# Windowed attention and a gated feed-forward on one core: the gate taken as a hyperbolic tangent from the exponential's table

## The chip, the cores and the metric

The kernel runs on one core of a Trainium2 chip. The metric is the device time of one execution in microseconds (us); the number given for a kernel is the median of several runs. A core has five engines that work side by side and wait for each other through semaphores: TensorE (PE, matrix products), VectorE (DVE), ScalarE (ACT, functions from a table, copies), GpSimd (POOL) and SyncE (SP, which here issues the transfers). In the profile, PEld is PE's loading of weights, which overlaps its products.

## The reference

Causal attention in a window of 64 positions (8 batches, 8 heads, 576 positions, 64 wide), then a gated feed-forward on 4608 tokens of width 512 with 1536 hidden elements.

```python
scores = np.where(mask, scores, -1000000000.0)
scores = scores - np.max(scores, axis=-1, keepdims=True)
attn = np.exp(scores)
attn = attn / (np.sum(attn, axis=-1, keepdims=True) + 1e-09)
...
gate = 1.0 / (1.0 + np.exp(-(x @ w_gate)))
val = x @ w_val
return (gate * val @ w_out).astype(np.float32)
```

x is the attention's output. The kernel needs two functions from ScalarE's table: the exponential in the softmax and the sigmoid in the gate.

## The kernel before

**Tiling.** The 4608 tokens are 12 token tiles `t` of 384. The attention of a tile is done in four units `(t, p)`, one for each pair of heads `p`. A unit has these steps: loads of q, k (L180, L181) and v (L191); `scores` (L210, PE); `exponentials` (L230), in which for each of two halves and three blocks DVE finds a minimum (L244) and ACT takes an exponential (L252); `normalize` (L262), where DVE takes the reciprocal of the row sums (`invert`, L259 and L260) and POOL or DVE multiplies by it (L269); `stage_b` (L296), in which PE transposes (L301) and ACT copies (L306, tile `pT`); and `outputs` (L325), the product with v (L331).

**Products in two ways.** Tiles 0 and 1 go through `up_gate`, `up_val` and `down`: for each of 12 hidden tiles `j`, PE computes a bank `ph` (L362) for the gate and one for the value, ACT makes the gate `g` from the first (`gate_table`, L371), DVE multiplies the second with it (L395) and splits the result into a high and a low part (L387, L389), and PE adds `down` (L409). There are three banks `ph`, taken in turn: a new bank's product waits until what read the bank three before is done. The other ten tiles go in pairs, in five stages `s`. A stage has six steps `k` of seven products (`product`, L613, matmuls at L586, tile `pr`), whose sums DVE combines (L596, L625); from them again a gate on ACT (L371) and a product on DVE (L629), four of each per step. Then follow the down products `y` (L586 too, from `last_product`), with `h_split` (L668 on ACT, L669 on DVE) ahead of them.

**Weights.** The weights come as 64-bit numbers and are converted in the kernel during the first 180 us: loads L105, on ACT L117, L118 and L158, on DVE L126 to L130 and L159, and stores to DRAM (L154, L448, L457). Sums of weights for the later stages are made on POOL (L508 to L528) from transfers back (L498).

**What sets the order.** The steps are put into a list of planned times, sorted and written out in that order (`put`, `attend`, L705 to L922). The tile framework then schedules each engine's instructions by a simulated timeline. PE's products keep the order of the program (`pe`, L85). ACT's exponentials and gates are held to one common order by `chain` and `table_order` (L88): each is issued after the one before, whichever of the two functions it is. Some steps are held behind a mark by hand (`marks`): exponentials of the first units behind an earlier `pT`; conversions of hidden tile `j` behind `marks[j]`, the last gate or exponential and the last split of an earlier tile; and the rounding of x (L576) behind the last gate.

**Table loads.** ScalarE has one table active at a time. Ahead of an instruction whose function isn't in the active table, the compiler puts a table load, which the profile shows under the line of that instruction: L252 for an exponential, L371 for a gate, L77 for the warm-up at the start.

Of the kernel before, what the change touches and what calls it, by code (L numbers as in the profile page):

```python
# [14 lines left out]
AF = mybir.ActivationFunctionType  # L15
ALU = mybir.AluOpType
# [10 lines left out]
def attn_ffn(ctx: ExitStack, tc: tile.TileContext, qT, kT, vN, w_gate, w_val, w_out, out, outT):  # L27
# [3 lines left out]
    nc = tc.nc  # L31
# [47 lines left out]
    def psum(s, i, nm):  # L79
        return ps_b.tile([P, DM], F32, name=nm, tag=f"b{s % 2}{i}")  # L80

    marks = {"pT": {}}
    chain = []
# [4 lines left out]
    def table_order():  # L88
        return tc.issue_after(chain[-1]) if chain else nullcontext()
# [166 lines left out]

    def invert(rs):

        nc.vector.scalar_tensor_tensor(out=rs, in0=rs, scalar=1e-9, in1=rs, op0=ALU.add, op1=ALU.max)  # L259
        nc.vector.reciprocal(out=rs, in_=rs)  # L260

    def normalize(t, p, h):  # L262
        pt, rs = st[(t, p, h)], sums_of[(t, p)][:, h, :]
        if t < 2 and h:
            nc.vector.reduce_sum(out=rs, in_=pt, axis=mybir.AxisListType.X)
        if t < 4:
            invert(rs)
        eng = nc.vector if t == 3 and p % 2 or t // 2 == 2 else nc.gpsimd
        eng.tensor_mul(out=pt, in0=pt, in1=rs.unsqueeze(2).broadcast_to([P, UP, P]))  # L269
# [21 lines left out]
    def stage_n(t, p):  # L291
        invert(sums_of[(t, p)])
        for h in range(2):
            normalize(t, p, h)
# [58 lines left out]
    def up(t, j, m):  # L353
        ph = h_bank(f"ph{m}_{t}_{j}")
        w2 = wgv[m][j]
        prs = []
        for p in range(NP):
            whi, wlo = (w2[:, p // 2, e, p % 2 * P:(p % 2 + 1) * P] for e in range(2))
            xh, xl = xs[(t, p)][:, 0, :], xs[(t, p)][:, 1, :]
            prs += [(whi, xh), (whi, xl), (wlo, xh)]  # L360
        for i, (l, r) in enumerate(prs):
            pe(nc.tensor.matmul(ph, l, r, start=i == 0, stop=i == len(prs) - 1))  # L362
        return ph
# [3 lines left out]

    def gate_table(t, j, c):
        g = mp.tile([P, TT], F32, name=f"g_{t}_{j}", tag="g", bufs=4)
        with table_order():  # L370
            act = nc.scalar.activation(g, c, AF.Sigmoid)  # L371
        chain.append(act.ins)
        marks["gate"] = act.ins
        gates[(t, j)] = g

    def up_gate(t, j):
        gate_table(t, j, up(t, j, 0))

    def hidden_split(t, j, h32, eng):
        if t == 1 and j < NF - KEEP:  # L380
            pool, tag, bufs = (xp, f"x{10 + j}", 1) if j < 4 else (xp, f"e{j - 4}", 1) if j < 9 else (mp, "raw", RAW)
            h2 = pool.tile([P, 2, TT], F32R, name=f"h2_{t}_{j}", tag=tag, bufs=bufs)
            h_hi, h_lo = h2[:, 0, :], h2[:, 1, :]
        else:
            h_hi = mp.tile([P, TT], F32R, name=f"hh_{t}_{j}", tag="hh", bufs=3)
            h_lo = mp.tile([P, TT], F32R, name=f"hl_{t}_{j}", tag="hl", bufs=3)
        nc.vector.tensor_copy(out=h_hi, in_=h32)  # L387
        hh[(t, j)] = (h_hi, h_lo)
        return eng.tensor_sub(out=h_lo, in0=h32, in1=h_hi.bitcast(F32))  # L389

    def up_val(t, j):
        ph = up(t, j, 1)
        g = gates.pop((t, j))
        h32 = mp.tile([P, TT], F32, name=f"h32_{t}_{j}", tag="c", bufs=CB)
        nc.vector.tensor_mul(out=h32, in0=ph, in1=g)  # L395
        last = hidden_split(t, j, h32, nc.vector)
        if t == 0:
            marks[j] = (chain[-1], last.ins)

    def down(t, j, i, first, last):  # L400
        h_hi, h_lo = hh[(t, j)]
# [28 lines left out]
    gates = {}  # L430
# [152 lines left out]
    def three(ps, w2, q, x2, first, last, check=True):  # L583
        whi, wlo = (w2[:, e, q * P:(q + 1) * P] for e in range(2))
        for i, (l, r) in enumerate(((whi, x2[:, 0, :]), (whi, x2[:, 1, :]), (wlo, x2[:, 0, :]))):
            pe(nc.tensor.matmul(ps, l, r, start=first and i == 0, stop=last and i == 2,  # L586
                                skip_group_check=not check))

    def combine(st, n, nm, emit):


        ps = st[PRODUCTS[n][2]][:, :TT]

        def plus(a, tag, bufs):
            o = mp.tile([P, TT], F32, name=f"{tag}{n}_{nm}", tag=tag, bufs=bufs)
            marks["plus"] = nc.vector.tensor_add(out=o, in0=ps, in1=a).ins  # L596
            return o

        if n == 0:
            st["p1"] = mp.tile([P, TT], F32, name=f"p1_{nm}", tag="p1", bufs=2)  # L600
            nc.scalar.copy(st["p1"], ps)
        elif n == 1:
            st["u2"] = plus(st["p1"], "u", 2)
        elif n == 3:
            emit(1, 1, st[2][:, :TT], plus(st["p1"], "c", CB))
        elif n == 4:
            emit(0, 0, ps, None)
        elif n == 5:
            emit(1, 0, ps, st["p1"])
        elif n == 6:  # L610
            emit(0, 1, ps, st["u2"])

    def product(s, k, n, m):  # L613
        st, b = acc[m], PRODUCTS[n][2]
        if n < 3:
            st[b] = psum(1 + m, b, f"pr{b}_{m}_{s}_{k}")
        for c in range(2):
            three(st[b][:, :TT], wt[(s, k, m, n)], c, xs[(s, n, c)][0], n < 3 and c == 0, c == 1, n < 3)

        def emit(r, b, in0, in1):  # L620
            t, j = 2 * s + b, k + r * NK
            c = in0
            if in1 is not None:
                c = mp.tile([P, TT], F32, name=f"c{n}_{m}_{s}_{k}", tag="c", bufs=CB)
                nc.vector.tensor_add(out=c, in0=in0, in1=in1)  # L625
            if m == 0:
                gate_table(t, j, c)
            else:
                nc.vector.tensor_mul(out=hidden(s, k)[2 * r + b], in0=c, in1=gates.pop((t, j)))  # L629

        combine(st, n, f"{m}_{s}_{k}", emit)

    def hidden(s, k):

        if (s, k) not in ht:
            nm = f"{s}_{k}"

            def one(tag, bufs, i):
                return mp.tile([P, TT], F32, name=f"h{i}_{nm}", tag=tag, bufs=bufs)

            def two(pool, tag, bufs, i):
                h2 = pool.tile([P, 2, TT], F32, name=f"h{i}_{nm}", tag=tag, bufs=bufs)
                return [h2[:, 0, :], h2[:, 1, :]]

            if k < 2:
                h5 = wts.tile([P, 5, TT], F32, name=f"h_{nm}", tag=f"wp_{k}")
                t = [h5[:, i, :] for i in range(5)]
            elif k == 2:
                t = [one("hh", 3, i) for i in range(3)] + [one("hl", 3, i) for i in range(3, 5)]
            else:  # L650
                t = two(mp, "raw", RAW, 0) + two(mp, "raw", RAW, 1)
                if k == 3:
                    t.append(one("hl", 3, 2))
                else:
                    if k == 4:
                        ht[(s, "last")] = two(wts, f"wo_{WOB}", 1, 2)
                    t.append(ht[(s, "last")][k - 4])
            ht[(s, k)] = t
        return ht[(s, k)]
# [66 lines left out]
    for n in range(2 * NP):  # L726
        t, p = divmod(n, NP)
# [32 lines left out]
    for i, (kind, t, j) in enumerate(plan):  # L760
        attend(i)
        at[(kind, t, j)] = now
        if (kind, t, j) == ("up", 0, 0):
            now = -9.9
        if kind == "up":
            put(now, 9, up_gate, t, j)
            now += UPT / 2
            attend(i + 0.5)
            put(now, 9, up_val, t, j)
            now += UPT / 2  # L770
        else:
            for x in range(TB):
                put(now + x * DPT, 9, down, t, j, x, j == 0, j == NF - 1)
            now += DNT
        if (kind, t, j) == ("up", 0, 0):
            now = 0.0
    for i in range(KINDS * NF):
        j, m = divmod(i, KINDS)
# [125 lines left out]
    for tm, _, f, a in events:  # L904
        if f in (conv_a, conv_b, conv_c):
            with ExitStack() as behind:
# [4 lines left out]
                j, m = divmod(a[0], KINDS)  # L911
# [56 lines left out]
```

## Time and profile before

| what | value |
|---|---|
| median of three runs | 962.8 us (959.86 to 964.3) |
| the profiled execution, and its span | 961.67 us, 959.9 us |
| busy in the span: PE, PEld | 941.3, 898.0 us |
| busy in the span: DVE, ACT, POOL | 714.3, 602.7, 147.5 us |
| mean granted TensorE clock | 0.998 |
| ACT table loads at L371, at L252, at L77 | 40, 39, 1 |
| DMA | 273.45 MB, mean 285 GB/s |

The span runs from the first to the last instruction. A row of the profile's groups reads: line, engine, operation, what is written and read, shapes, count | busy us, mean ns of one | idle time of the engine just before, and what ended it. In a timeline, a row starts with its start and its duration in us, and square brackets hold the idle time of the engine ahead of it. In a list of waits stand the total, the number and the longest.

### The profile page before, as it was taken

Reading aid. Unit: us, or ns where it says so; the run is one execution under the profiler, and the core shown is the slowest. Engines: PE = TensorE matmul, PEld = TensorE weight load, DVE = VectorE, ACT = ScalarE, POOL = GpSimd, SP = SyncE. Lnnn points to the kernel's source line nnn. Section 1 sums busy time; section 2 is a strip of 40 time slices with the busy share of each in tenths; the row PEclk is TensorE's granted clock in tenths of the full one; section 3 lists DMA queues with packets and bytes.
Section 4 is the critical chain, followed back from the end, with each engine's and each line's share of the span. In section 5 each row is a group of like instructions: output and inputs, shape, how many; then the busy total and the mean of one; then the engine's idle time right before and its main releaser. Section 6 shows DMA issues by size and latency. Waiting matters only on the chain.

```text
span 959.9 us, 20420 instructions
## 1 busy us (share of the span) xinstructions
PE 941.3 (98%) x7164; PEld 898.0 (94%) x7164; DVE 714.3 (74%) x1919; ACT 602.7 (63%) x1487; POOL 147.5 (15%) x232
## 2 busy tenths in 40 slices
PE   6899999999999999999999999999999999999998
PEld 5799998879998999999999999999999999999998
DVE  7898989788778985666976576796566697567782
ACT  7878878667677754766755666764666675222350
POOL 4210103703765000110100111100110100000000
PEclk9999999999999999999999999999999999999999
DMA  9899988979988999888889888879988868988464
GB/s 339 304 357 370 347 303 271 347 275 358 369 301 271 402 325 309 277 265 269 251 260 316 267 273 261 270 256 284 302 273 249 268 220 257 314 249 251 143 217 157
DMA packets 105510, 273.45 MB, mean 285 GB/s; under 512 B 11456, under 2 KB 33600, under 8 KB 105408
## 3 DMA queue, kind: packets, MB, share of 16 engines
q1 hardware_dynamic: 105408, 272.15, 84.7%
q8 instruction: 57, 0.93, 0.4%
q14 instruction: 45, 0.37, 0.1%
HBM read 220.20 MB, written 51.90 MB: 283 GB/s over the span
## 4 chain that ended last, share of the span: by engine, by line
PE 77%; ACT 6%; DVE 5%; DMA 5%; issue 3%; POOL 2%; SPq 0%; DVEq 0%; ACTq 0%; POOLq 0%
PE pr L586 42%; PE y L586 23%; PE s L220 3%; PE pp L301 2%; PE ph L362 2%; PE y L409 2%; DMA w32d<-w 2%; PE s L331 2%; ACT p L252 2%; DMA a<-w32d 1%; PE oo L331 1%; DVE w L130 1%; POOL ws L528 1%; ACT L252 1%; ACT raw L118 1%
## 5 line engine op out<-in xcount | busy, mean ns | idle before, releaser
L586 PE MATMUL pr<-x_T,wt 128*128 128x384 f32 x1224 | 227.5, 338 | 0.0
L586 PE MATMUL y<-h,wot 128*128 128x384 f32 x1260 | 219.9, 334 | 0.0
L586 PEld LDWEIGHTS y<-h,wot 128*128 128x128 f32 x1260 | 218.2, 188 | 0.6 <-DVE h L629 0.3
L586 PEld LDWEIGHTS pr<-x_T,wt 128*128 128x128 f32 x1224 | 211.6, 188 | 4.5 <-issue 3.6
L586 PE MATMUL pr<-x_B,wt 128*128 128x384 f32 x1008 | 189.4, 336 | 0.0
L586 PEld LDWEIGHTS pr<-x_B,wt 128*128 128x128 f32 x1008 | 174.7, 188 | 0.8 <-issue 0.5
L668 ACT CAST h<-h 128x384 fp32r<-128x384 f32 x210 | 102.7, 515 | 80.6 <-PE y L586 43.3
L269 POOL TENSOR_TENSOR p<-p,rs 128x384 f32<-128x384 f32 x76 | 66.4, 890 | 551.8 <-DVE rs L260 496.7
L669 DVE TENSOR_TENSOR h<-h,h 128x384 fp32r<-128x384 f32 x210 | 110.7, 554 | 26.8 <-ACT h L668 26.1
L252 ACT ACTIVATE p<-p,mn 128x128 f32<-128x128 f32 x288 | 110.9, 393 | 10.2 <-DVE mn L244 9.7
L362 PE MATMUL ph<-x,w 128*128 128x384 f32 x576 | 107.0, 339 | 1.3 <-ACT g L371 0.8
L362 PEld LDWEIGHTS ph<-x,w 128*128 128x128 f32 x576 | 99.5, 188 | 4.3 <-ACT g L371 1.4
L371 ACT ACTIVATE g<-c 128x384 f32<-128x384 f32 x90 | 46.6, 524 | 66.3 <-DVE c L625 65.9
L244 DVE CUSTOM_DVE_ANT_0 p<-s,m 128x128 f32<-128x128 f32 x288 | 65.3, 284 | 27.6 <-PE s L220 27.5
L629 DVE TENSOR_TENSOR h<-c,g 128x384 f32<-128x384 f32 x90 | 55.5, 616 | 30.2 <-ACT g L371 24.7
L371 ACT ACT_TABLE_LOAD x40 | 51.3, 1283 | 12.7 <-DVE c L625 11.4
L220 PE MATMUL s<-k,q 64*64 64x128 f32 x1152 | 46.5, 293 | 7.2 <-DMA k<-in_kT_dram 5.8
L596 DVE TENSOR_TENSOR c<-pr,p 128x384 f32<-128x384 f32 x60 | 33.0, 550 | 23.7 <-PE pr L586 23.7
L252 ACT ACT_TABLE_LOAD x39 | 50.0, 1283 | 0.7
L252 ACT ACTIVATION_READ_ACCUMULATOR p<-p,mn 128x1 f32 x264 | 49.8, 188 | 0.0
L220 PEld LDWEIGHTS s<-k,q 64*64 64x64 f32 x1152 | 34.2, 141 | 13.9 <-DMA q<-in_qT_dram 5.2
L301 PE MATMUL pp<-ident,p 128*128 128x128 f32 x288 | 42.6, 281 | 4.6 <-POOL p L269 2.6
(106 smaller groups left out, 1215.9 us busy)
## 6 DMA issues: line engine op xcount, KB each, us to landing
wt<-wd SPq DMA_DIRECT2D x186, 512.0 KB, 4.5
wot<-wod SPq DMA_DIRECT2D x105, 512.0 KB, 4.7
v<-in_vN_dram SPq DMA_DIRECT2D x48, 384.0 KB, 5.4
wd<-ws SPq DMA_DIRECT2D x48, 256.0 KB, 4.4
k<-in_kT_dram SPq DMA_DIRECT2D x48, 224.0 KB, 5.2
q<-in_qT_dram SPq DMA_DIRECT2D x48, 192.0 KB, 5.1
w32d<-w SPq DMA_DIRECT2D x36, 256.0 KB, 4.6
wd<-w SPq DMA_DIRECT2D x36, 256.0 KB, 5.8
```

The source lines that it names most:

```text
L220: pe(nc.tensor.matmul(sc[h][half * BLK:(half + 1) * BLK, u, :], qt[h * BLK:(h + 1) * BLK, U * BLK:(U + 1) * BLK], kt[h * BLK:(h + 1) * BLK ...
L244: nc.vector.tensor_tensor_reduce(out=pt[:, u, :], in0=sc[:, u, :], in1=masks[key], op0=ALU.add, op1=ALU.min, scale=-SCALE, scalar=3.0e38, ...
L252: exp = nc.scalar.activation(pt[:, u, :], pt[:, u, :], AF.Exp, bias=mn[:, u:u + 1], scale=-1.0, **sums)
L269: eng.tensor_mul(out=pt, in0=pt, in1=rs.unsqueeze(2).broadcast_to([P, UP, P]))
L301: pe(nc.tensor.transpose(pp[:, u, :], pt[:, u, :], ident))
L362: pe(nc.tensor.matmul(ph, l, r, start=i == 0, stop=i == len(prs) - 1))
L371: act = nc.scalar.activation(g, c, AF.Sigmoid)
L586: pe(nc.tensor.matmul(ps, l, r, start=first and i == 0, stop=last and i == 2, skip_group_check=not check))
L596: marks["plus"] = nc.vector.tensor_add(out=o, in0=ps, in1=a).ins
L629: nc.vector.tensor_mul(out=hidden(s, k)[2 * r + b], in0=c, in1=gates.pop((t, j)))
L668: nc.scalar.copy(h2[:, 0, :], src)
L669: nc.vector.tensor_sub(out=h2[:, 1, :], in0=src, in1=h2[:, 0, :].bitcast(F32))
```

## The change

The gate becomes `AF.Tanh` in place of `AF.Sigmoid`, and one plus the tangent is multiplied with the value in one instruction of DVE (`gated`, a scalar-tensor-tensor: add 1, then multiply) in place of the plain product. For this to be the same number, x must come in half: sigmoid(z) = (1 + tanh(z/2))/2, and gate and value are both linear in x. The half is taken in the softmax: `invert` now takes the reciprocal of twice the sum plus 2e-9. The exponentials stay in `chain`; the gates are taken out of it, so that ACT's order of gates against exponentials is left to the scheduler.

```diff
     def invert(rs):
-        nc.vector.scalar_tensor_tensor(out=rs, in0=rs, scalar=1e-9, in1=rs, op0=ALU.add, op1=ALU.max)
+        nc.vector.scalar_tensor_tensor(out=rs, in0=rs, scalar=2e-9, in1=rs, op0=ALU.add, op1=ALU.add)
         nc.vector.reciprocal(out=rs, in_=rs)
...
     def gate_table(t, j, c):
         g = mp.tile([P, TT], F32, name=f"g_{t}_{j}", tag="g", bufs=4)
-        with table_order():
-            act = nc.scalar.activation(g, c, AF.Sigmoid)
-        chain.append(act.ins)
+        act = nc.scalar.activation(g, c, AF.Tanh)
         marks["gate"] = act.ins
         gates[(t, j)] = g
+
+    def gated(out, val, g):
+        nc.vector.scalar_tensor_tensor(out=out, in0=g, scalar=1.0, in1=val, op0=ALU.add, op1=ALU.mult)
...
-        nc.vector.tensor_mul(out=h32, in0=ph, in1=g)
+        gated(h32, ph, g)
         last = hidden_split(t, j, h32, nc.vector)
         if t == 0:
-            marks[j] = (chain[-1], last.ins)
+            marks[j] = (marks["gate"], last.ins)
...
-                nc.vector.tensor_mul(out=hidden(s, k)[2 * r + b], in0=c, in1=gates.pop((t, j)))
+                gated(hidden(s, k)[2 * r + b], c, gates.pop((t, j)))
```

In the changed kernel the gate stands at L370, the product at L375, and what follows is one line lower or higher than before. ACT keeps the one table load of the warm-up. PE and POOL keep their order; on SP one pair of transfers trades places (a store of weight parts, L448, and a load for the sums, L498).

On ACT around the exponentials of attention unit (4, 2), in the first of the five stages, stood before (`xf` is a tile of x, `p` the scores that become weights, `mn` and `rs` minima and sums, `g` a gate, `c` a combined product):

```order
L285 COPY xf_0_3282<-s_4_2_3269 128x128
L252 ACT_TABLE_LOAD
L252 ACTIVATE p_4_2_3297,rs_2_3299<-p_4_2_3297,mn_4_2_3298 128x128 x3
L288 COPY xf_0_3282<-s_4_2_3268 128x128
L252 ACTIVATE p_4_2_3307,rs_2_3299<-p_4_2_3307,mn_4_2_3308 128x128 x3
L371 ACT_TABLE_LOAD
L371 ACTIVATE g_6_3333<-c_0_1_0_3331 128x384
```

and stand now:

```order
L285 COPY xf_0_3282<-s_4_2_3269 128x128
L252 ACTIVATE p_4_2_3297,rs_2_3299<-p_4_2_3297,mn_4_2_3298 128x128 x3
L288 COPY xf_0_3282<-s_4_2_3268 128x128
L252 ACTIVATE p_4_2_3307,rs_2_3299<-p_4_2_3307,mn_4_2_3308 128x128 x3
L370 ACTIVATE g_6_3333<-c_0_1_0_3331 128x384
```

The two table loads are gone and nothing else moved; this is how it looks in nearly all units. On ACT around the exponentials of unit (2, 3), while the last weights are converted, stood before (`raw` is a loaded weight, `w` a converted one):

```order
L371 ACTIVATE g_9_2273<-ph_0_9_2260 128x384
L158 CAST w_10_2279<-w_1_10_2247 128x2x256
L252 ACT_TABLE_LOAD
L252 ACTIVATE p_2_3_2302,rs_3_2304<-p_2_3_2302,mn_2_3_2303 128x128 x3
L252 ACTIVATE p_2_3_2314,rs_3_2304<-p_2_3_2314,mn_2_3_2315 128x128 x3
L117 ACTIVATE w_0_11_2401<-raw_11_2348 128x512
L118 ACTIVATE raw_11_2348<-raw_11_2348 128x512
L118 ACTIVATE raw_11_2361<-raw_11_2361 128x512
L118 ACTIVATE raw_10_2381<-raw_10_2381 128x512
```

and stand now:

```order
L370 ACTIVATE g_9_2273<-ph_0_9_2260 128x384
L118 ACTIVATE raw_11_2348<-raw_11_2348 128x512
L118 ACTIVATE raw_11_2361<-raw_11_2361 128x512
L118 ACTIVATE raw_10_2381<-raw_10_2381 128x512
L158 CAST w_10_2279<-w_1_10_2247 128x2x256
L117 ACTIVATE w_0_11_2401<-raw_11_2348 128x512
L252 ACTIVATE p_2_3_2302,rs_3_2304<-p_2_3_2302,mn_2_3_2303 128x128 x3
L252 ACTIVATE p_2_3_2314,rs_3_2304<-p_2_3_2314,mn_2_3_2315 128x128 x3
```

Four instructions of the conversion now stand ahead of the exponentials. On DVE at the same unit stood before (`rs` are the sums whose reciprocal is taken, `h` the product with the gate, `hh` and `hl` its parts, `zz` a step of the conversion):

```order
L259 SCALAR_TENSOR_TENSOR rs_3_2304<-rs_3_2304 128x3
L395 TENSOR_TENSOR h_0_9_2338<-ph_0_9_2325,g_9_2273 128x384
L130 ISA w_2_9_2285<-raw_9_2209,w_2_9_2285 128x1024
L260 RECIPROCAL rs_3_2304<-rs_3_2304 128x3
L259 SCALAR_TENSOR_TENSOR rs_3_2304<-rs_3_2304 128x3
L387 CAST hh_9_2340<-h_0_9_2338 128x384
L260 RECIPROCAL rs_3_2304<-rs_3_2304 128x3
L389 TENSOR_TENSOR hl_9_2341<-h_0_9_2338,hh_9_2340 128x384
L126 TENSOR_SCALAR zz_11_2422<-w_0_11_2401 128x512
L128 SCALAR_TENSOR_TENSOR w_0_11_2401<-w_0_11_2401,zz_11_2422 128x512
```

and stand now:

```order
L375 SCALAR_TENSOR_TENSOR h_0_9_2338<-g_9_2273,ph_0_9_2325 128x384
L130 ISA w_2_9_2285<-raw_9_2209,w_2_9_2285 128x1024
L388 CAST hh_9_2340<-h_0_9_2338 128x384
L259 SCALAR_TENSOR_TENSOR rs_3_2304<-rs_3_2304 128x3
L390 TENSOR_TENSOR hl_9_2341<-h_0_9_2338,hh_9_2340 128x384
L126 TENSOR_SCALAR zz_11_2422<-w_0_11_2401 128x512
L260 RECIPROCAL rs_3_2304<-rs_3_2304 128x3
L259 SCALAR_TENSOR_TENSOR rs_3_2304<-rs_3_2304 128x3
L128 SCALAR_TENSOR_TENSOR w_0_11_2401<-w_0_11_2401,zz_11_2422 128x512
L260 RECIPROCAL rs_3_2304<-rs_3_2304 128x3
```

The product with the gate and the conversion come first now, the two reciprocals after them, the second one last. Unit (3, 2) is changed in the same way, with two conversions among the exponentials.

## The prediction

> **What bounds the kernel now.** I read the page first, its busy times.
>
> ```profile
> PE 941.3 (98%) x7164; PEld 898.0 (94%) x7164; DVE 714.3 (74%) x1919; ACT 602.7 (63%) x1487; POOL 147.5 (15%) x232
> ```
>
> TensorE (PE) is busy 98% of the span of 959.9 us, while ScalarE (ACT), the engine that the change relieves, is busy 63%. A share is an average, so I cut the span into stretches: one with the first attention units, one with tiles 0 and 1 and the first stage of products, one with the later product stages, and the end.
>
> ```profile
> 0.00:40.00 40.00, 30.23 (x416) 24.55 (x418) 29.36 (x157) 32.35 (x105) 16.40 (x28) 0.96 0.89 327
> 40.00:320.00 280.00, 274.86 (x2133) 251.93 (x2130) 237.46 (x637) 212.12 (x506) 90.56 (x156) 1.00 0.93 326
> 320.00:920.00 600.00, 600.00 (x4417) 585.59 (x4416) 430.79 (x1094) 347.78 (x856) 40.51 (x48) 1.00 0.83 269
> 920.00:960.00 40.00, 36.22 (x209) 35.90 (x208) 16.74 (x34) 10.49 (x22) 0.00 (x0) 1.00 0.59 197
> ```
>
> After the stretch and its length come the busy times of PE, of PE's weight loads (PEld), VectorE (DVE), ACT and GpSimd (POOL), then PE's clock, the DMA share and GB/s. From 320 to 920 us PE is busy for all of the 600 us. The first 40 us lack 9.8 us, the last 40 us 3.8 us, and the 280 us between them 5.14 us; the clock is full from 40 us on. Matmul ends are modelled, so "all busy" needs a second look. The chain of waits gives it: in that stretch it runs through PE, piece after piece.
>
> ```profile
> 477.50 43.88 PE y L586 x252
> 629.27 43.88 PE y L586 x252
> ```
>
> That is 174 ns a matmul (43.88/252), the same in both, and a stage of 151.8 us from one piece to the next (629.27 - 477.50). So the later stages are bound by TensorE's own work, and the time to be had lies in PE's waits. Last view: PE's waits from 35 us (just ahead of the first gate) to 320 us; none is listed after that.
>
> ```profile
> PE pp L301 <- DVE p L269: 1.9, 3, 1.3
> PE ph L362 <- ACT g L371: 0.8, 2, 0.4
> PE ph L362 <- DVE h L395: 0.6, 1, 0.6
> PE oo L331 <- ACT pT L306: 0.5, 1, 0.5
> PE s L220 <- DMA k<-in_kT_dram: 0.5, 1, 0.5
> PE pp L301 <- POOL p L269: 0.4, 1, 0.4
> PE s L220 <- ACT xf L319: 0.2, 1, 0.2
> ```
>
> Together 4.9 us in ten waits (total, times, longest).
>
> **The change part by part.** First, what leaves and what takes its place:
>
> ```profile
> L371 ACT ACT_TABLE_LOAD x40 | 51.3, 1283 | 12.7 <-DVE c L625 11.4
> L252 ACT ACT_TABLE_LOAD x39 | 50.0, 1283 | 0.7
> L252 ACT ACTIVATE p<-p,mn 128x128 f32<-128x128 f32 x288 | 110.9, 393 | 10.2 <-DVE mn L244 9.7
> L371 ACT ACTIVATE g<-c 128x384 f32<-128x384 f32 x90 | 46.6, 524 | 66.3 <-DVE c L625 65.9
> L629 DVE TENSOR_TENSOR h<-c,g 128x384 f32<-128x384 f32 x90 | 55.5, 616 | 30.2 <-ACT g L371 24.7
> L395 DVE TENSOR_TENSOR h<-ph,g 128x384 f32<-128x384 f32 x24 | 13.2, 550 | 0.1
> L128 DVE SCALAR_TENSOR_TENSOR w<-w,zz 128x512 int32<-128x512 int32 x36 | 25.1, 697 | 0.4
> L159 DVE TENSOR_TENSOR w<-w,w 128x512 fp32r<-128x512 f32 x36 | 25.9, 723 | 2.9 <-ACT w L158 2.9
> ```
>
> 1. *Table loads.* The new order has one, the warm-up's; 40 + 39 = 79 go, 79 x 1.283 = 101 us of ACT. In the 600 us in which PE never waits this buys nothing by itself: it turns into idle time of ACT. It counts where a table load stands ahead of something that PE waits for. I went through the ten waits.
>
> The longest is the 1.3 us one, of attention unit (4, 2) (token tile, head pair):
>
> ```profile
> 285.77 1.28 ACT L252 ACT_TABLE_LOAD   x1
> 289.67 1.28 ACT L371 ACT_TABLE_LOAD   x1
> 286.28 0.08 DVE L244 DVE_READ_ACCUMULATOR2_ANT mn<- 128x1 f32 x1
> 289.69 0.17 DVE L259 SCALAR_TENSOR_TENSOR rs<-rs 128x6 f32<-128x6 f32 x1 [1.33 <-ACT p L252]
> 290.43 0.65 DVE L269 TENSOR_TENSOR p<-p,rs 128x384 f32<-128x384 f32 x1
> 291.52 0.70 DVE L629 TENSOR_TENSOR h<-c,g 128x384 f32<-128x384 f32 x1 [0.45 <-ACT g L371]
> 292.15 0.81 DVE L269 TENSOR_TENSOR p<-p,rs 128x384 f32<-128x384 f32 x1
> 293.10 0.52 PE L301 MATMUL pp<-ident,p 128*128 128x128 f32 x3 [1.28 <-DVE p L269]
> ```
>
> PE's second three transposes wait for the second normalization L269, which stands on DVE behind the gate's product L629, which waits for the gate, which stands behind the second table load; the reciprocal (L259) waits for exponentials that stand behind the first. Without the first, the exponentials can start when the first minimum is there (286.28 + 0.08 = 286.36, against 285.77 + 1.28 = 287.05 for the end of the load), some 0.7 us earlier; without the second the gate follows by another 1.28 us, and DVE would end the second L269 about 1.3 us earlier. PE's own time to reach these transposes is 293.10 - 1.28 = 291.8, so all 1.28 us go, with little to spare.
>
> The wait for L395, at unit (3, 1), goes only in part:
>
> ```profile
> 174.75 0.94 DVE L159 TENSOR_TENSOR w<-w,w 128x512 fp32r<-128x512 f32 x1
> 175.96 0.16 DVE L259 SCALAR_TENSOR_TENSOR rs<-rs 128x3 f32<-128x3 f32 x1 [0.27 <-ACT p L252]
> 176.04 0.55 DVE L395 TENSOR_TENSOR h<-ph,g 128x384 f32<-128x384 f32 x1
> 176.64 2.36 PE L362 MATMUL ph<-x,w 128*128 128x384 f32 x12 [0.55 <-DVE h L395]
> ```
>
> DVE stood for 0.27 us ahead of L259; the rest of the 0.55 us is DVE's own weight conversion. I take 0.27.
>
> The other waits that a table load precedes I cost at their full length: the two gates (0.8), the rest of the L269 row on DVE (1.9 - 1.28 = 0.6), POOL's L269 (0.4) and pT (0.5, its copy is queued behind the first gate). The k load (0.5) and xf (0.2) have none ahead of them and stay. Sum: 1.28 + 0.27 + 0.8 + 0.6 + 0.4 + 0.5 = 3.85 us.
>
> 2. *Order.* On PE and POOL nothing moves. The freed order moves several instructions at two places, units (3, 2) and (2, 3): ACT takes weight conversions ahead of exponentials, DVE takes the reciprocals later. What is queued behind them is POOL's normalization, then PE's transposes; first (3, 2), then (2, 3):
>
> ```profile
> 115.99 1.94 POOL L269 TENSOR_TENSOR p<-p,rs 128x384 f32<-128x384 f32 x2 [14.04 <-DVE rs L259]
> 121.17 0.82 PE L301 MATMUL pp<-ident,p 128*128 128x128 f32 x6
> 153.66 1.94 POOL L269 TENSOR_TENSOR p<-p,rs 128x384 f32<-128x384 f32 x2 [14.90 <-DVE rs L259]
> 160.68 0.82 PE L301 MATMUL pp<-ident,p 128*128 128x128 f32 x6
> ```
>
> They have 121.2 - 117.9 = 3.2 us and 160.7 - 155.6 = 5.1 us to spare. At (2, 3) the second reciprocal is now behind a subtraction (hl), a zz and an L128 more, each at most about 0.7 us by these rows, so some 2 us; at (3, 2) behind the first two of them. On ACT the conversions ahead take the place of the table load that went. I cost the move at nothing; if that cover were gone, every further microsecond would be PE's. The swapped pair on the SP queue (a store of parts and a load for the sums) is costed at nothing for the same reason.
>
> 3. *Gate and product.* No row shows a hyperbolic tangent. The nearest rows are the sigmoid at 524 ns and, at a third of the elements, the exponential, 393 ns with a bias operand: a tangent at either's speed changes nothing, and one twice as slow would cost 144 x 0.52 = 75 us of ACT (144 gates, 12 token tiles by 12 hidden tiles), less than the 101 us set free. The product as a scalar-tensor-tensor: by L128 and L159, 697 against 723 ns at 512 elements, it costs what the plain one did, 550 to 616 ns at 384; I take no difference, with 10% either way, 144 x 0.06 = 9 us of DVE, which has 42 us idle between 40 and 320 us and 169 us after that. The reciprocal keeps its number of instructions.
>
> 4. *What is late next.* PE arrives up to 3.9 us earlier at everything, but weights, sums and k come by DMA, whose share is 0.93 between 40 and 320 us. Some of the time will be waited for there instead. No row gives the amount; it lies between 0 and 3.85 us. As conversions on ACT come earlier as well, I take little, 0.35 us.
>
> **Sum:** 3.85 - 0.35 = 3.5 us. The profiled execution took 961.67 us, its span plus 1.8 us around it: 961.67 - 3.5 = **958.2 us**. That execution lies 1.1 us below the median of the runs shown, 962.8, and inside their spread (959.86 to 964.3); from the median the same sum gives 959.3. A measurement of this kernel tells about 0.5%, 4.8 us, from no change, so the forecast is a gain that lies below that bound.
>
> **The rivals.** *More is hidden than the waits show.* If PE idle on the list is only the visible part, all 5.14 us between 40 and 320 us go. Beyond them there are weight loads that stand idle where PE does not, after 320 us:
>
> ```profile
> PEld s L331 <- issue: 3.7, 15, 0.3
> PEld s L331 <- ACT g L371: 1.5, 6, 0.3
> ```
>
> With the 1.5 us that these owe to the gate, 5.1 + 1.5 = 6.6 us, 955.0 us. For it: each wait also drains PE's pipeline. Against it: the same weight load idles by as much at "issue", with no gate behind it (3.7/15 = 0.25 us, as 1.5/6). [...] I hold the rival at 29%.
>
> *The gain is eaten by DMA.* PE waits for k, weights or sums by what it gained: 961.7 us. For it: the DMA share and the k load on the list. Against it: none of PE's waits after 35 us but 0.5 us is for a transfer. 13%.
>
> *The product is slow.* The one way I see to the other side: DVE takes a scalar-tensor-tensor of floats much slower than the plain product. 24 + 24 products (tiles 0 and 1, and the first product stage) fall between 40 and 320 us, where DVE idles 280 - 237.5 = 42.5 us: 0.89 us each. From there on the excess is PE's, since its banks ph and pr are freed by these products. At three times the plain price, 1.1 us extra, 48 x 0.21 = 10 us less the 3.5: 968.3 us. The pair 697 and 723 ns speaks against it. 6%.
>
> *It doesn't do what it says*, and loads remain in other places: the order of the changed kernel on ACT has a single one, so I leave this out.
>
> **How the numbers follow.** Forecast, 958.2 us: 52%. Hidden gain, 955.0: 29%. Eaten, 961.7: 13%. Slow product, 968.3: 6%. Faster by over 0.5% is the second case, 0.29; within 0.5% the first and the third, 0.65; slower the last, 0.06. The range leaves out the last case and goes from 955.0 to 961.7 us plus what the median lies above the profiled execution, to 963.0.
>
> **What would show it.** ACT: one table load, ACT about 100 us less busy, gates near 520 ns. DVE: products near 550 to 616 ns. PE: of the ten waits only the k load, xf and a part of L395 stand; PE still busy for all of the later stages. The forecast is wrong if the 4.9 us of waits return under other names, above all DMA, or if the stages of 151.8 us become shorter, which would say that a "busy" PE had been held by ACT.

## The result, and the profile after

| | before | after |
|---|---|---|
| median (lowest to highest), us | 962.8 (959.86 to 964.3), five runs | 954.68 (953.44 to 956.07), five runs |
| profiled execution, and its span, us | 961.67, 959.9 | 955.21, 953.4 |
| ratio of the times, 95% interval | 1 | 0.9924 (0.9908 to 0.994) |

The changed kernel is 0.76% faster, 7.3 us by the ratio (0.0076 x 962.8), and the two medians are 8.1 us apart; the interval, 0.6 to 0.92%, lies wholly above the 0.5% bound. The span of the profiled execution is 6.5 us shorter. The forecast was 3.5 us and "within 0.5%". The median lies 0.3 us below the lower end of the range, at the number given for the rival "more is hidden than the waits show". That end was counted from the profiled execution of before, and the profiled execution after, 955.21 us, lies 0.2 us above it.

First the page's busy times after, and its two rows for the gate and the gated product:

```profile
PE 938.2 (98%) x7164; PEld 898.0 (94%) x7164; DVE 721.7 (76%) x1919; ACT 507.0 (53%) x1408; POOL 155.3 (16%) x232
...
L370 ACT ACTIVATE g<-c 128x384 f32<-128x384 f32 x90 | 47.0, 522 | 85.4 <-DVE c L626 79.5
...
L375 DVE SCALAR_TENSOR_TENSOR h<-g,c 128x384 f32<-128x384 f32 x90 | 53.6, 595 | 6.3 <-ACT g L370 0.9
```

ACT has 79 instructions fewer (1487 to 1408) and is 95.7 us less busy. A gate takes 522 ns where the sigmoid took 524, a product 595 ns where the plain one took 616. None of the three explains 6.5 us: ACT was not the bound, and the other two hardly moved.

Next the same cuts of the span as before; columns are the busy times of PE, PEld, DVE, ACT and POOL, then the clock, the DMA share and GB/s.

```profile
0.00:40.00 40.00, 30.23 (x418) 24.63 (x420) 29.81 (x158) 31.79 (x105) 16.41 (x28) 0.96 0.88 327
40.00:320.00 280.00, 278.23 (x2184) 257.57 (x2179) 247.70 (x652) 180.79 (x486) 93.25 (x156) 1.00 0.95 338
320.00:920.00 600.00, 600.00 (x4401) 586.42 (x4401) 433.88 (x1091) 288.18 (x806) 45.65 (x48) 1.00 0.83 266
```

Between 40 and 320 us PE fitted 2184 matmuls in place of 2133, so the gain is made there. Equal stretches of time hold different work, though. A better cut holds the same work: from the product `ph` (L362) that follows PE's wait at 41 us to the start of the first down products `y`, 2139 matmuls in both; first before, then after:

```profile
42.16:325.71 283.55, 278.94 (x2139) 255.90 (x2137) 241.26 (x645) 215.75 (x512) 90.56 (x156) 1.00 0.93 329
```

```profile
41.81:319.62 277.81, 276.29 (x2139) 255.84 (x2137) 245.54 (x647) 179.55 (x483) 93.25 (x156) 1.00 0.95 338
```

This stretch is 5.74 us shorter, and two columns give two accounts of it. By PE its idle time fell from 4.61 to 1.52 us, 3.09 us. By PEld the busy time stayed the same (255.90 and 255.84), and the idle time fell from 27.65 to 21.97 us, 5.68 us: the whole gain.

PE's waits from 35 to 320 us after the change, against the ten (4.9 us) of before:

```profile
PE s L220 <- DMA k<-in_kT_dram: 0.8, 1, 0.8
PE pp L301 <- DVE p L269: 0.5, 1, 0.5
PE oo L331 <- ACT pT L306: 0.3, 1, 0.3
PE s L220 <- ACT xf L319: 0.2, 1, 0.2
```

Every wait for a gate, for the product of a gate and for POOL is gone, and so is the 1.28 us one. The later stages, in the chain of waits after:

```profile
319.62 43.88 PE y L587 x252
471.26 43.88 PE y L587 x252
...
905.78 43.98 PE y L587 x252
```

A stage is now 151.64 us from one piece to the next, against 151.77 before: 0.13 us each, in stages in which PE is "all busy" in both. In all, 6.1 us had been gained when the first `y` begins (325.71 to 319.62), and 0.4 us in what follows: 0.13 us in each of three stages, and nothing in the last one, which takes 131.24 us from `y` to `y` in both.

### The profile page after: what moved, and what is told of

Read it like the earlier page. It is cut to its first block, busy times and chain, and to the rows that moved or that the text cites. A ratio compares the mean times of both kernels' runs of the same rounds, so it can differ in the third digit from the quotient of the medians.

```text
span 953.4 us, 20341 instructions
## 1 busy us (share of the span) xinstructions
PE 938.2 (98%) x7164; PEld 898.0 (94%) x7164; DVE 721.7 (76%) x1919; ACT 507.0 (53%) x1408; POOL 155.3 (16%) x232
## 4 chain that ended last, share of the span: by engine, by line
PE 92%; DMA 3%; DVE 2%; issue 0%; SPq 0%; ACT 0%; POOL 0%; DVEq 0%; ACTq 0%
PE pr L587 44%; PE y L587 23%; PE ph L362 11%; PE y L410 4%; PE s L220 4%; PE pp L301 3%; PE s L331 2%; PE oo L331 1%; DMA wa<-w32d 1%; PE pr L331 1%; DMA wod<-wa 1%; DMA k<-in_kT_dram 1%; DMA a<-w32d 1%; DVE p L244 0%; SPq L464 0%
## 5 line engine op out<-in xcount | busy, mean ns | idle before, releaser
L269 POOL TENSOR_TENSOR p<-p,rs 128x384 f32<-128x384 f32 x76 | 72.5, 970 | 545.3 <-DVE rs L260 377.5
L362 PE MATMUL ph<-x,w 128*128 128x384 f32 x576 | 106.3, 339 | 0.0
L362 PEld LDWEIGHTS ph<-x,w 128*128 128x128 f32 x576 | 99.6, 188 | 2.1 <-issue 1.0
L370 ACT ACTIVATE g<-c 128x384 f32<-128x384 f32 x90 | 47.0, 522 | 85.4 <-DVE c L626 79.5
L375 DVE SCALAR_TENSOR_TENSOR h<-g,c 128x384 f32<-128x384 f32 x90 | 53.6, 595 | 6.3 <-ACT g L370 0.9
L602 ACT COPY p<-pr 128x384 f32<-128x384 f32 x60 | 28.8, 480 | 54.1 <-PE pr L587 54.1
L306 ACT COPY pT<-pp 128x384 f32<-128x384 f32 x96 | 41.3, 482 | 30.0 <-PE pp L301 29.5
```

What stands on the lines that cost most here:

```text
L306: cp = nc.scalar.copy(pT, pp)
L370: act = nc.scalar.activation(g, c, AF.Tanh)
L375: nc.vector.scalar_tensor_tensor(out=out, in0=g, scalar=1.0, in1=val, op0=ALU.add, op1=ALU.mult)
```

## The experiments

The change has three parts that could be at work: the table loads that go, the order that is freed, the new product. Five kernels take them apart, the rest measure what loads cost at chosen places. Beside single times stands the start of the first `y` pieces in the profile, which divides the gain into what comes before 320 us and the stages behind. Landmarks of one trace must not be read too finely: kernels that agree up to a place differ there by some tenths of a microsecond, and once, below, by 1.8.

**Loads gone, order as before** (e1: the changed kernel with the gates back in `chain`)

```diff
-        act = nc.scalar.activation(g, c, AF.Tanh)
+        with table_order():
+            act = nc.scalar.activation(g, c, AF.Tanh)
+        chain.append(act.ins)
```

> The changed kernel with the gates put back into the one order of exponentials and gates, so that every engine's order is that of the kernel before and only the table loads are gone (and the product is the new one). Theory A (the loads stood ahead of what TensorE waited for): as the changed kernel, a span of 953.4 us within 1 us, ratio to before 0.992 to 0.994. Rival B (the freed order brings the gain): near the kernel before, span 959 to 960.5 us, ratio above 0.997.

Measured: 955.28 us, ratio 0.993 (0.9914 to 0.9945), span 954.1; the first `y` starts at 320.28 us, and a stage takes 151.64. That is the changed kernel's time to within both intervals. Loads that go are enough, and the free order is not needed.

**Order free, loads kept** (e2: the kernel before with the gates out of `chain`; sigmoid, plain product and reciprocal as before)

```diff
-        with table_order():
-            act = nc.scalar.activation(g, c, AF.Sigmoid)
-        chain.append(act.ins)
+        act = nc.scalar.activation(g, c, AF.Sigmoid)
```

> The kernel before with the gates taken out of the common order and nothing else: the sigmoid, its 79 loads and the plain product stay, the order on every engine is that of the changed kernel. A: a span of 959 to 960.5 us, ratio 0.998 to 1.002. B: 953 to 955 us, ratio below 0.995.

**The new product alone** (e3: the kernel before with a scalar-tensor-tensor that adds 0)

```diff
-        nc.vector.tensor_mul(out=h32, in0=ph, in1=g)
+        nc.vector.scalar_tensor_tensor(out=h32, in0=g, scalar=0.0, in1=ph, op0=ALU.add, op1=ALU.mult)
```

> The kernel before with the product taken as a scalar-tensor-tensor (add 0, then multiply), sigmoid, loads and order as before. A: no change, span 959.5 to 960.5 us, ratio 0.998 to 1.002. Rival C (the new product frees VectorE sooner and accounts for the part of the gain that TensorE's list of waits lacks, some 3 us): span 956.5 to 957.5 us, ratio 0.996 to 0.998.

Measured: 961.43 us, ratio 0.9998 (0.9988 to 1.0007) for the order, first `y` at 327.48; 961.42 us, ratio 0.9995 (0.9986 to 1.0005) for the product, first `y` at 326.22. Neither does anything that the times can tell; one reading missed what was expected, e2's profiled span of 961.7 us for at most 960.5. The row of e3's product, between the same neighbours as before, next to the 616 ns of the plain one:

```profile
L377 DVE SCALAR_TENSOR_TENSOR h<-g,c 128x384 f32<-128x384 f32 x90 | 55.6, 617 | 30.1 <-ACT g L371 24.6
```

The new instruction costs what the old one did. That it reads 595 ns in the changed kernel, and 601 in e1, is not the instruction's own doing.

**Where in the program** (e4: tangent for tiles 0 to 3, that is up to the first product stage, sigmoid and `chain` after; e5: the reverse)

```diff
+    def half(t):
+        return t < 4        # e5: t >= 4
...
+        if half(t):
+            act = nc.scalar.activation(g, c, AF.Tanh)
+        else:
+            with table_order():
+                act = nc.scalar.activation(g, c, AF.Sigmoid)
+            chain.append(act.ins)
```

> Tangent gates for tiles 0 to 3 alone (the stretch up to about 320 us); from the second product stage on the sigmoid, the plain product and 47 of the 79 loads are back, in one chain with the exponentials. A: the down products of the first stage begin at 319.6 us as in the changed kernel, later stages take 151.8 us again in place of 151.6; span 953.9 us (953.4 to 954.4). Rival E (loads in the later stages hold a TensorE that looks busy): several us of the 6.5 are lost, span above 956.

> The reverse: sigmoid, plain product and chain for tiles 0 to 3, tangent gates without loads from the second product stage on. A: the down products of the first stage begin at 325.7 us as before, each later stage 0.14 us shorter; span 959.4 us (958.9 to 959.9). E: span below 957.

Measured: e4 954.47 us, ratio 0.9921 (0.9903 to 0.994); e5 961.23 us, ratio 0.9998 (0.9989 to 1.0008). The whole gain comes from the 32 loads of the first third; the 47 behind them are worth nothing that the time can tell. Their worth is small but visible in the chain of waits, e4 first, then e5:

```profile
319.20 43.88 PE y L601 x252
470.97 43.88 PE y L601 x252
```

```profile
325.99 43.88 PE y L601 x252
477.63 43.88 PE y L601 x252
```

With loads in the later stages the period is 151.76 to 151.80 us (before, e2, e3 and e4), without them 151.64 (e5, e1 and the changed kernel): 0.13 us a stage, whatever came ahead.

These chains also put an error on the 6.1 us. In the four kernels with no loads up to there (changed, e1, e4, and e10 below) the first `y` starts at 319.62, 320.28, 319.20 and 319.30 us, in the four with them (before, e2, e3, e5) at 325.71, 327.48, 326.22 and 325.99. The means are 319.60 and 326.35: 6.75 us, with 5.4 us between the nearest two.

**Loads put back at one place** (e6: 2, e7: 4 loads, by dummy sigmoids ahead of unit (4, 2)'s exponentials)

```diff
+    def reload(n):
+        for f in [AF.Sigmoid, AF.Exp] * (n - 1) + [AF.Sigmoid]:
+            with table_order():
+                chain.append(nc.scalar.activation(warm, warm, f).ins)
...
+        if (t, p, h) == (4, 2, 0):
+            reload(1)       # e7: reload(2)
```

> The changed kernel with two table loads put back at one place, ahead of the exponentials of unit (4, 2) (a sigmoid of one column that nothing uses brings them). ScalarE starts these exponentials 2.8 us later, of which 0.6 us is covered by the first minimum. A: TensorE's second transposes there wait again, 1.3 to 1.7 us by the list of waits, and its next product stands 0.2 to 0.4 us more than that behind the changed kernel's time; nothing is recovered later: span 954.9 to 955.6 us. If a wait costs no more than its listed idle time, shift and idle time agree within 0.1 us.

> The same with four loads at that place (sigmoid, exponential, sigmoid on one column). A: 2.8 us more waiting than with two, listed idle 4.0 to 4.6 us, the shift again 0.2 to 0.4 us above the list whatever its length; span 957.6 to 958.6 us. Rival (the list is short by a share, as 4.9 listed against 6.1 gained): the excess grows to about 1 us.

Measured, one run each: 955.55 and 955.85 us, spans 953.7 and 953.9. Both miss their aim, for two reasons. The unit was wrong: the 1.28 us wait, which the prediction put down to unit (4, 2), belongs to (4, 3); unit (4, 2) runs at some 226 us. And the scheduler put the dummy sigmoids far ahead of the place meant, as the timelines of ACT show, e6's, then e7's:

```profile
207.33 1.28 ACT L233 ACT_TABLE_LOAD   x1
...
224.66 1.28 ACT L259 ACT_TABLE_LOAD   x1
```

```profile
206.12 1.28 ACT L233 ACT_TABLE_LOAD   x1
...
208.67 1.28 ACT L233 ACT_TABLE_LOAD   x1
...
210.70 1.28 ACT L233 ACT_TABLE_LOAD   x1
...
212.61 1.55 ACT L420 COPY yo<-y 128x512 f32<-128x512 f32 x3
```

e6's two loads move the end by 0.3 us of span, no more than the traces scatter: its wait for k alone is 1.6 us where the changed kernel's is 0.8. In e7 three of the four loads stand ahead of a copy (`yo`) for which PE waits, at a place where the changed kernel has no wait; PE's row, then PEld's:

```profile
213.24 1.31 PE L594 MATMUL pr<-x_B,wt 128*128 128x384 f32 x6 [1.57 <-ACT yo L420]
```

```profile
213.24 1.00 PEld L594 LDWEIGHTS pr<-x_B,wt 128*128 128x128 f32 x6 [1.89 <-ACT yo L420]
```

PE loses 1.84 us there (from 1.14 ahead of the changed kernel to 0.70 behind). The end is only 0.5 us later because e7 was ahead when it came to this place. PE's list holds 1.57 of what was lost, PEld's 1.89. (The expectation for e8, below, puts these loads where TensorE doesn't depend on them; of e7's that isn't so.) e6 also shows that a tangent needs no exponential's load ahead of it: behind the sigmoid's load at 207.33 us its gates at 221.07 and 221.62 us (0.53 and 0.49 us) run with none, and the next load comes at 224.66 us.

**The same, held at unit (4, 3)** (e8: 2 loads, e9: 4 loads, behind the last copy of `xf`)

```diff
+    def reload(n, behind):
+        for f in [AF.Sigmoid, AF.Exp] * (n - 1) + [AF.Sigmoid]:
+            with table_order(), tc.issue_after(behind):
+                chain.append(nc.scalar.activation(warm, warm, f).ins)
...
-            nc.scalar.copy(x[:, 1, :], oo[1])
+            last = nc.scalar.copy(x[:, 1, :], oo[1]).ins
+            if (t, p) == (4, 3):
+                reload(1, last)     # e9: reload(2, last)
```

> The changed kernel with two table loads put back at one place, ahead of the exponentials of unit (4, 3), held behind the copies of x that stand there (the two runs before had theirs at another unit, and the scheduler drew most of them forward, to where TensorE doesn't depend on them). The exponentials and the gate behind them come 2.8 us later than in the changed kernel, against 2.6 us in the kernel before. A: TensorE waits at that unit's transposes as before or a little more, 1.3 to 1.7 us by its own list and 0.2 us more by the list of its weight loads; what follows stands later than in the changed kernel by what the weight loads' list says, 1.5 to 1.9 us, and nothing of it is recovered: span 954.8 to 955.5 us. If TensorE's own list holds the whole price, shift and list agree within 0.1 us.

> The same with four loads there, 3.0 us more. A: shift 4.4 to 5.0 us, again the weight loads' idle time, and again some 0.2 us above TensorE's own list (a fixed amount for a wait, not a share of it): span 957.6 to 958.5 us.

e8, one run: 956.15 us, span 954.4. PE's step at this place, the scores of the next unit against the changed kernel, is +1.13 us (from 0.15 ahead to 0.98 behind), less than expected, and the end is 1.0 us later. PE's timeline of e8 around the transposes, with the idle time ahead in brackets, then PEld's:

```profile
287.41 0.52 PE L308 MATMUL pp<-ident,p 128*128 128x128 f32 x3 [0.54 <-DVE p L269]
288.13 0.52 PE L308 MATMUL pp<-ident,p 128*128 128x128 f32 x3 [0.21 <-DVE p L269]
```

```profile
287.38 0.31 PEld L308 LDWEIGHTS pp<-ident,p 128*128 128x128 f32 x3 [0.83 <-ACT p L609]
288.10 0.31 PEld L308 LDWEIGHTS pp<-ident,p 128*128 128x128 f32 x3 [0.42 <-issue]
```

A wait made on purpose at a known place: PE lists 0.75 us of it, PEld 1.25, and the program lost 1.13. PE's list is too short by 0.4 us, PEld's too long by 0.1.

e9, one run: 958.05 us, span 956.3. The step at the place is +4.68 us, as large as expected; the total is not, because this run was 1.8 us ahead of the changed kernel when it came there, by steps at places that the edit doesn't touch. And the step isn't made as expected. The waits, PE's and PEld's:

```profile
288.09 1.46 PE L308 MATMUL pp<-ident,p 128*128 128x128 f32 x6 [2.89 <-DVE p L269]
```

```profile
288.06 1.09 PEld L308 LDWEIGHTS pp<-ident,p 128*128 128x128 f32 x6 [3.18 <-ACT g L377]
```

They explain 3.2 us. The other 1.5 us are in the clock, the third number from the end of each row in e9's cut:

```profile
287.00:288.00 1.00, 0.00 (x0) 0.00 (x0) 1.00 (x3) 1.00 (x3) 0.00 (x0) 1.00 0.93 381
288.00:288.50 0.50, 0.41 (x3) 0.44 (x3) 0.50 (x2) 0.50 (x2) 0.00 (x0) 0.67 0.30 123
...
289.00:290.00 1.00, 1.00 (x6) 1.00 (x5) 1.00 (x3) 0.84 (x2) 0.00 (x0) 0.50 0.01 4
...
291.50:292.00 0.50, 0.50 (x4) 0.50 (x4) 0.50 (x2) 0.00 (x0) 0.00 (x0) 0.92 0.43 156
292.00:294.00 2.00, 2.00 (x23) 1.75 (x23) 0.41 (x1) 0.87 (x2) 0.60 (x2) 1.00 0.00 0
```

Six transposes take 1.46 us in place of 0.82. So e9 can't serve as the doubled dose of e8, and the price of a load is not read from it.

**The k load earlier** (e10: one transfer, of unit (5, 0)'s k, ahead of a store on SP)

```diff
-    LOAD_AHEAD = 8
+    LOAD_AHEAD = 9
```

> The changed kernel with attention loads planned one unit of time earlier; the one move in any engine's order is that the k load of unit (5, 0) goes ahead of a store of weight sums on the SP queue, behind which it stood. A: TensorE's wait for k there, 0.8 us, the longest that is left after the first gate, becomes 0 to 0.2 us, and the down products of the first stage begin 0.5 to 1 us earlier than at 319.6 us; ratio to the kernel before 0.9905 to 0.9930, not to be told from the changed kernel's 0.9924. Rival: the load waits for the transfers themselves, and the wait stays.

Measured: 954.85 us, ratio 0.9909 (0.989 to 0.9928); PE's wait for k is 0.4 us in place of 0.8, and the first `y` starts at 319.30 in place of 319.62, both less than expected (0 to 0.2 us for the wait, 0.5 to 1 us for `y`). The time can't be told from the changed kernel, and the shorter wait is no proof either: the same wait is 1.5 us in e1, 1.1 in e4, 1.6 in e6 and 0.5 in e9, none of which moves that load. No version was found that beats the changed kernel.

## Why the prediction was right and wrong

**Right: what bounds the kernel, and what does the work.** The later stages are PE's own work, and their loads turned into idle time of ACT, all but 0.13 us a stage (e4, e5). The gain is made ahead of 320 us, at waits of PE that table loads had caused (e1). The order (e2), the scalar-tensor-tensor (e3) and the tangent (522 ns) cost nothing, as they were costed.

**Wrong: the size of the sum, 3.85 us for what turned out to be 6.1 in this pair of traces and 6.75 in the mean of eight.** The step that failed is the pricing of the ten waits by PE's own list. The wait for POOL, costed at 0.4 us, shows why. Before, PE's timeline, then PEld's:

```profile
101.09 0.49 PE L301 MATMUL pp<-ident,p 128*128 128x128 f32 x3
102.00 0.55 PE L301 MATMUL pp<-ident,p 128*128 128x128 f32 x3 [0.42 <-POOL p L269]
```

```profile
102.00 0.31 PEld L301 LDWEIGHTS pp<-ident,p 128*128 128x128 f32 x3 [0.65 <-POOL p L269]
```

and PE's after:

```profile
100.57 0.82 PE L301 MATMUL pp<-ident,p 128*128 128x128 f32 x6
```

Six transposes in one piece take 0.82 us, in two pieces 0.49 + 0.55 = 1.04. The 0.22 us between the two comes with the break (three more in the same piece add 0.82 - 0.49 = 0.33 us, three behind the wait take 0.55), and PE's rows call it busy. With the 0.42 that makes 0.64, which is what PEld shows as idle (0.65), and what the program gained at this place (PE's lead over before grows by 0.65 us here). The same holds at the 1.28 us wait: 0.49 + 0.52 - 0.82 = 0.19 more, 1.47 in all; PEld shows 1.49, and the step is 1.47.

```profile
291.34 0.49 PE L301 MATMUL pp<-ident,p 128*128 128x128 f32 x3
```

```profile
293.07 0.31 PEld L301 LDWEIGHTS pp<-ident,p 128*128 128x128 f32 x3 [1.49 <-ACT p L601]
```

PEld's rows of before at the two gates and at L395:

```profile
158.46 2.06 PEld L362 LDWEIGHTS ph<-x,w 128*128 128x128 f32 x12 [0.63 <-ACT g L371]
```

```profile
176.64 2.04 PEld L362 LDWEIGHTS ph<-x,w 128*128 128x128 f32 x12 [0.99 <-DVE h L395]
...
179.44 2.06 PEld L362 LDWEIGHTS ph<-x,w 128*128 128x128 f32 x12 [0.77 <-ACT g L371]
```

Term by term, in us; the step is by how much PE's lead over before grows at that place, read where PE runs without a gap again:

| wait of before | the term | idle of PEld | step |
|---|---|---|---|
| second transposes, unit (4, 3) | 1.28 | 1.49 | 1.47 |
| product of a gate, L395, unit (3, 1) | 0.27 | 0.99 | 0.81 |
| two gates | 0.8 | 0.63 + 0.77 | 0.61 + 0.74 |
| POOL, L269 | 0.4 | 0.65 | 0.65 |
| sum | 2.75 | 4.53 | 4.28 |

- *The 1.28 us wait* was named unit (4, 2); it is (4, 3). The two loads and their place in the queue were read rightly. e8 puts two loads back there and loses 1.13 us, so most of that step is theirs; that all of it is, the runs don't show.
- *L395* was cut from 0.55 to 0.27 because DVE's conversion (L159) stands ahead of it. But that conversion doesn't stay where it was: after the change the rows on DVE read

```profile
172.18 0.94 DVE L159 TENSOR_TENSOR w<-w,w 128x512 fp32r<-128x512 f32 x1
...
173.38 0.54 DVE L375 SCALAR_TENSOR_TENSOR h<-g,ph 128x384 f32<-128x384 f32 x1
```

L159 comes 2.57 us earlier (174.75 to 172.18), PE here came only 1.81 us earlier with what it had gained so far, so DVE was no longer late. Whatever stands ahead of a wait has its own share of the gain. Nor does this wait hang on loads alone: e8, whose two loads come only at 280 us, has it again, 0.3 us by PE.
- *The rest of L269 on DVE* (0.6) went only in part: of its two waits the one of 0.47 us stayed in full in the changed kernel, as the list after shows, so no load is needed for it (it is not on the lists of e1 and e10, which have no loads either). The other, 0.17 us by PE at 249.24 us, went; PEld was idle for 0.46 us there, and the step is 0.51. *pT* (0.5) went to 0.3, ahead of this stretch.
- Together the four rows give 4.28 us of the 5.74, and this last wait 0.51. The other 0.95 us is the sum of steps of at most 0.4 us to both sides, among them the wait for k, which takes back 0.3. Some gains are at places where only PEld lists a wait before (0.37 and 0.35 us at two units' products with v); one by one they are too close to the scatter to be put down to loads.

**Given back to DMA, 0.35 us:** PE's wait for k grew by 0.3 us (0.5 to 0.8), as forecast, but the kernels give it anything up to 1.6 us: with loads in this stretch 0.5 (before), 1.0 (e2), 1.1 (e3) and none on the list (e5), without them 0.4 to 1.5. The step isn't refuted, only not shown.

**The rival that came.** "More is hidden than the waits show" was held at 29% with 955.0 us. Its reason was right for the stretch ahead of 320 us and larger than it said (5.7 us and more, for 5.1); its 1.5 us for the later stages was wrong. That its sum, 6.6 us, comes so near to the 6.5 us of the spans is in part luck: the first term was 1.0 us too small (5.1 for 6.1), the second 1.1 us too large (1.5 for 0.4). In the later stages PEld's waits after, beside the two rows of before that the prediction shows, list:

```profile
PEld s L331 <- issue: 5.2, 21, 0.3
```

The six waits for a gate (1.5 us) are gone, and the 3.7 us at "issue" in 15 places have become 5.2 in 21: the same idle time under another name, as the prediction argued.

The prediction named one more sign of being wrong: later stages that become shorter, which would say that a "busy" PE had been held by ACT. By 0.13 us a stage this sign came, and the trace of before shows the place, in the second stage on ACT, DVE and PEld:

```profile
426.50 1.28 ACT L371 ACT_TABLE_LOAD   x1
```

```profile
428.35 0.75 DVE L629 TENSOR_TENSOR h<-c,g 128x384 f32<-128x384 f32 x1 [1.45 <-ACT g L371]
...
430.67 1.01 DVE L596 TENSOR_TENSOR u<-pr,p 128x384 f32<-128x384 f32 x2
```

```profile
431.27 2.06 PEld L586 LDWEIGHTS pr<-x_T,wt 128*128 128x128 f32 x12 [0.17 <-DVE u L596]
```

The gate stands behind the load, its product L629 waits for the gate, the sum `u` is queued behind L629, and a weight load of PE waits for `u`; PE's own rows show no idle time there. PEld lists this wait once in each of three stages in the four kernels with loads there (before, e2, e3, e4) and in none of the others, and it is at this product that the stages gain their 0.13 us.

The argument against the rival was made from these late waits, and then carried over to the early ones, where a wait is a real one and 0.2 to 0.4 us more are lost on top of it, which is what the runs show of the drain that the rival named.

The two readings of TensorE's idle time part here. In the early stretch the weight loads' is the one that agrees with the gain (5.68 us of PEld's idle against 5.74 gained, and 3.09 by PE); in the later stages PEld's 14.4 us of idle before the change (600 - 585.59) was hardly room, since it still has 13.6 us there (600 - 586.42).

**Not so:** the slow product (617 ns against 616), and the gain eaten by DMA.

## What to carry to other kernels

Price a wait of TensorE by the idle time of its weight loads, not by the matmuls' own: at each real wait here a further 0.2 to 0.4 us was lost that counts as busy. Where loads were put back, PEld's idle time came within 0.1 us of what PE lost (1.25 for 1.13 in e8, 1.89 for 1.84 in e7), and PE's own fell short (0.75 and 1.57); e9, where the clock fell too, is the exception. Take for real a wait that names another engine and breaks a run of matmuls in two; one that turns into "issue" when its releaser goes was none. And when several waits in a row go, don't hold fixed what stands ahead of the next one, since it moves as well.

## What the hardware showed that was not expected

After TensorE had idled for about 3 us (2.89 by PE, 3.18 by PEld) in e9, its clock fell to one half just as it took up work. By an estimate that takes the clock as either full or half, its means of 0.67 from 288.0 to 288.5 and of 0.92 from 291.5 to 292.0 put the half clock from 288.17 to 291.58 us, 3.41 us long, which costs 1.7 us of work: 4 table loads (5.1 us of ACT) at a bad place cost half as much again as the wait for them by PEld (4.68 us for 3.18). After the 1.28 us of idle (1.49 by PEld) in the kernel before the clock stayed full, and so it did after e7's 1.57 us (1.89 by PEld); first before, then e7:

```profile
293.00:294.00 1.00, 0.90 (x7) 0.93 (x8) 1.00 (x2) 0.89 (x3) 1.00 (x2) 1.00 1.03 291
```

```profile
213.00:214.00 1.00, 0.76 (x4) 0.76 (x5) 1.00 (x3) 1.00 (x3) 0.00 (x0) 1.00 0.07 25
```

Idle times between these and e9's were not tried, and e9 is one run: from what idle time on the clock falls, and whether idle time alone brings it down, is not shown.
